# Even transforms of an FFT-and-FFN kernel: the middle chunk as two products of 64 rows, with a PSUM bank for each sum

## The chip, the cores and the metric

The kernel runs on one core of a Trainium2 chip. The metric is the device time of one execution in microseconds (us). TensorE (PE, with its weight loads as PEld) multiplies, VectorE (DVE), ScalarE (ACT) and GpSimd (POOL) do the elementwise work, SyncE (SP) issues most transfers.

## The reference

A two-dimensional FFT of a real array of 8 x 3072 x 256, of which the real part is kept, and a feed-forward layer on its 24,576 rows, all in 32-bit floats:

```python
def _attn_ref(x):
    X = np.fft.fft(x, axis=1)
    X = np.fft.fft(X, axis=2)
    return X.real.astype(np.float32)

def _moe_ref(x, w_in, w_out, alpha):
    h = x @ w_in                      # 256 -> 2048
    g = np.maximum(h, 0.0) + alpha * np.minimum(h, 0.0)
    return (g @ w_out).astype(np.float32)
```

## The kernel before, in words

The FFT along the features is folded into `w_in`, the one along the sequence is folded by symmetries and then done as products with tables of cosines and sines. Of each of the 8 batches come four blocks of 2 x 384 columns (386 in the first); each block goes through the feed-forward layer in 16 steps (`KF`), one for each 128 hidden features. So there are 64 steps to a batch, numbered r = 0 to 63, and s counts them through the whole program. The order of the work is written out by hand: a step emits `ffn1(s + 3)` (six products into two PSUM banks, lines 648 to 650, called q = 0 and q = 1 below), `ffn2(s)` (twelve products into the four accumulators `acc`, line 727) and `pair(s + 3)` with the elementwise work of the steps around it: DVE adds up `pf` (line 666) and `d` (line 673), ACT scales `d` back into the bank (line 677, tile `pq`), DVE makes `g` of both (line 631, in `split`), ACT rounds `g` to `hi` (line 633), POOL takes the rest `lo` (line 635). A bank of `ffn1` is free again when `split` has made its `g`.

Beside this, in each batch, the next batch's input is folded (`fold_piece`, r = 5 to 50) and transformed. The change is in the transforms of the even part, the *units* `see` (at r = 53), `cee` and then `ceo` (both at r = 57) and `seo` (r = 59); for batch 0 they stand in the prologue (`see`, `cee`) and at r = 10 and 11 (`ceo`, `seo`). A unit has three chunks of 128 rows of folded input, `fe[:, o]` to `fe[:, o + 2]`. The even sum needs the first chunk and half of the rows of the middle one, the odd sum the other half of the middle one and the last. Before, the middle chunk is multiplied twice with all 128 rows, with tables (`tab[:, 1]`, `tab[:, 2]`) whose other half is zero; so a unit has four products in 32-bit floats (`cee` a fifth, of the row `zres`), each of 192 or 193 columns, and both sums lie side by side in one bank (`ps`, line 510). Then `unit` calls `split` for the first bank of the step whose `g` is still open, ACT copies the odd sum to `os` (line 517), DVE makes `y` from the even sum plus and minus `os` (lines 525, 526), and ACT and POOL round `y` into `x` (lines 561, 562).

The four PSUM banks of the pool `pq` are shared by `ffn1` and the transforms. A new tile takes the bank whose release stands earliest in the program, and its first product waits for that release.

The 8-column case `m < P` of the same function (tile `f`) is the transform of one input column, done once for all batches.

Of the kernel before, what the change touches and what calls it, by code (L numbers as in the profile page):

```python
# [9 lines left out]
F32 = mybir.dt.float32  # L10
# [6 lines left out]
ACTF = mybir.ActivationFunctionType  # L17
ALU = mybir.AluOpType

NB, N, D, DFF = 8, 3072, 256, 2048  # L20
P = 128
# [92 lines left out]
def fft2_prelu_ffn(ctx: ExitStack, tc: tile.TileContext, t, out_a, out_b):  # L114
    nc = tc.nc
# [10 lines left out]
    pq = ctx.enter_context(tc.tile_pool(name="pq", bufs=4, space=PSUM))  # L126
    accp = ctx.enter_context(tc.tile_pool(name="accp", bufs=1, space=PSUM))
    ctx.enter_context(tc.manual_schedule())
    start = ctx.enter_context(ExitStack())
    st = start.enter_context(tc.tile_pool(name="st", bufs=1))  # L130

    V, S, G = nc.vector, nc.scalar, nc.gpsimd
# [10 lines left out]
    ee = tabs.tile([P, 9, 193], F32, name="ee")  # L143
# [63 lines left out]
    def other_bank():  # L207

        for s, i in list(st1):
            if i == 0 and s >= WHOLE:  # L210
                split(s, i)
        return pq.tile([P, 512], F32, tag="pq", name="ps")
# [145 lines left out]
    def fold_sums(i):  # L358

        b, c, h = PIECES[i]  # L360
        r = buf["x", i].rearrange("p (j i) s d -> p i s j d", i=2)
        ps = accp.tile([P, 512], F32, tag=f"acc{i % 4}", name="fold")
        for k in range(2):
            for n, (i_, s_) in enumerate(((0, 0), (0, 1), (1, 0), (1, 1))):
                nc.tensor.matmul(
                    out=ps[:, 256 * k:256 * k + 256], lhsT=ident[:, k * (i_ ^ s_)], rhs=r[:, i_, s_],
                    start=(n == 0), stop=(n == 3),
                )
        use("x", i)
        halves = ps.rearrange("p (k a j d) -> p k j a d", k=2, a=2, j=2)  # L370
        v = foldp.tile([P, 2, 2, 64], F32, tag="xeg", name="xeg")
        S.activation(out=v, in_=halves[:, :, 1], func=ACTF.Copy)
        return halves[:, :, 0], v
# [73 lines left out]
    TABS = dict(cee=ee[:, 0:4], see=ee[:, 5:9], ceo=eo[:, 0:4], seo=eo[:, 4:8])  # L447
# [44 lines left out]
    def dft(kind, half, fe, fo, zr, m, bank=None):  # L492

        ps = (bank or other_bank())[0:m]
        if kind in TABS:
            tab = TABS[kind]
            n = 193 if kind[1:] == "ee" else 192
            o = 0 if kind[1:] == "ee" else 3
            even = [(fe[:, o], tab[:, 0]), (fe[:, o + 1], tab[:, 1])]
            if kind == "cee":  # L500
                even.append((zr, ee[:, 4]))
            oddp = [(fe[:, o + 1], tab[:, 2]), (fe[:, o + 2], tab[:, 3])]
        else:
            n = 192
            sl = slice(half * 192, (half + 1) * 192)
            even = [(fo[:, q], odd[:, q, sl]) for q in range(3)]
            oddp = [(fo[:, 3 + q], odd[:, 3 + q, sl]) for q in range(3)]
        for o, terms in ((0, even), (n, oddp)):
            for i, (lhsT, rhs) in enumerate(terms):
                nc.tensor.matmul(  # L510
                    out=ps[:, o:o + n], lhsT=lhsT, rhs=rhs, start=(i == 0), stop=(i == len(terms) - 1),
                )
        return ps, n, m

    def odd_sums(ps, n, m):
        os = foldp.tile([P, 193], F32, tag="os", name="os", bufs=2)[0:m, 0:n]
        S.activation(out=os, in_=ps[:, n:2 * n], func=ACTF.Copy)
        return ps, os, n, m

    def butterfly(ps, n, m):  # L520
        return both_sums(*odd_sums(ps, n, m))

    def both_sums(ps, os, n, m, pool=foldp, tag="y"):
        y = pool.tile([P, WX], F32, tag=tag, name="y", bufs=1 if tag == "pf" else 2)[0:m, 0:2 * n]
        V.tensor_tensor(out=y[:, 0:n], in0=ps[:, 0:n], in1=os, op=ALU.add)
        V.tensor_tensor(out=y[:, n:2 * n], in0=ps[:, 0:n], in1=os, op=ALU.subtract)  # L526
        return y

    X = {}
# [8 lines left out]
    def unit_mm(b, kind, half, bank=None):  # L538
        s = 0 if kind[0] == "c" else 2
        fe, fo = (fold[b, "ce"], fold[b, "co"]) if s == 0 else (fold[b, "se"], fold[b, "so"])  # L540
        return dft(kind, half, fe, fo, zres, P, bank)
# [59 lines left out]
    def column_128_mm(kind, half):  # L601
        return dft(kind, half, f128, None, z128, NB)
# [190 lines left out]
    sums = {0: fold_sums(0)}  # L793
# [19 lines left out]
    fold_rest(4, *sums[4])  # L813
    weights_ih(0)
    x_sums = odd_sums(*column_128_mm("cee", 0))
    weights_mm(1)
    signs()
# [3 lines left out]
    fold_rest(5, *sums[5])  # L821
    weights_m(2, G)
    see_sums = odd_sums(*unit_mm(0, "see", 0))
    column_128_store("cee", 0, both_sums(*x_sums, pool=work, tag="pf"))
    load_xbc(0)
    weights_ih(1)
    weights_out(1)
    cee_sums = unit_mm(0, "cee", 0)
    y = both_sums(*see_sums)
    unit_store(0, "see", 0, G, y)  # L830
    cee_sums = odd_sums(*cee_sums)
    weights_c(1)
    y = both_sums(*cee_sums)
# [126 lines left out]
```

## Time and profile before

| | |
|---|---|
| median of 3 runs | 1796.56 us (1795.61 to 1797.21) |
| the profiled execution | 1797.46 us, its span 1795.7 us |
| PE busy | 99% of the span |
| DVE, POOL, ACT busy | 86%, 75%, 65% |
| share of the chain that ended last | PE 95% |
| mean granted TensorE clock | 0.997 of full speed |

Busy shares are of the whole span. The chain is followed back from the last instruction to what released each step. PE's records overlap, since products are pipelined: the distance from one start to the next is what a product costs in a row of them, not its own duration.

### The profile page before, as it was taken

What the parts mean: (1) busy time and instruction counts of PE and PEld (TensorE: products, weight loads), DVE (VectorE), ACT (ScalarE), POOL (GpSimd) and SP (SyncE); (2) the same over time, 40 slices, a digit from 0 to 9 for tenths busy, and PEclk for the clock granted to TensorE, in tenths of its full rate; (3) what the DMA queues carried; (4) which work ended last, traced back from release to release, by engine and by line L of the source; (5) the groups of instructions that cost most, each with busy time, mean ns of one, the idle gap of its engine ahead of it and who ended that gap; (6) DMA issues with size and microseconds to landing.
All of it is one profiled execution on the core that took longest, in us unless ns stands there. A gap on an engine that the chain in (4) does not pass through costs nothing.

```text
span 1795.7 us, 31584 instructions
## 1 busy us (share of the span) xinstructions
PE 1775.4 (99%) x9969; PEld 1740.1 (97%) x9969; DVE 1538.5 (86%) x3033; ACT 1169.5 (65%) x2426; POOL 1345.3 (75%) x1534
## 2 busy tenths in 40 slices
PE   8999999999999999999999999999999999999999
PEld 7789999999999999999999999999999999999998
DVE  6978987999879897798987989789997999878886
ACT  5865666666666667666676666666666666666665
POOL 2369977888678887788777887778877888676665
PEclk9999999999999999999999999999999999999999
DMA  6410110110101100010100111001110100000000
GB/s 242 144 35 26 58 64 19 39 42 17 46 23 35 42 35 29 23 46 30 62 19 6 47 46 47 19 6 58 35 46 19 39 20 4 23 23 23 23 19 19
DMA packets 28764, 71.76 MB, mean 40 GB/s; under 512 B 6546, under 2 KB 11700, under 8 KB 28468
## 3 DMA queue, kind: packets, MB, share of 16 engines
q1 hardware_dynamic: 28020, 69.31, 11.3%
q8 instruction: 78, 1.28, 0.3%
q14 instruction: 90, 0.74, 0.1%
q10 hardware_dynamic: 576, 0.43, 0.1%
HBM read 44.45 MB, written 25.26 MB: 39 GB/s over the span
## 4 chain that ended last, share of the span: by engine, by line
PE 95%; DVE 2%; POOL 1%; issue 0%; ACT 0%; DVEq 0%; POOLq 0%; ACTq 0%
PE acc L727 58%; PE pq L648 10%; PE pq L649 10%; PE pq L650 10%; PE ps L510 3%; PE ps L467 2%; PE acc L714 2%; PE ps L289 1%; DVE g L631 1%; DVE d L673 0%; POOL lo L635 0%; DVE xev L356 0%; ACT hi L633 0%; DVE pf L666 0%; POOL w L258 0%
## 5 line engine op out<-in xcount | busy, mean ns | idle before, releaser
L635 POOL TENSOR_TENSOR lo<-g,hi 128x384 fp32r<-128x384 f32 (+1 forms) x996 | 1020.6, 1040 | 325.4 <-ACT hi L633 300.5
L633 ACT ACTIVATE hi<-g 128x384 fp32r<-128x384 f32 (+1 forms) x996 | 523.9, 526 | 477.7 <-DVE g L631 447.6
L631 DVE SCALAR_TENSOR_TENSOR g<-d,sg,pq 128x384 f32<-128x384 f32 (+1 forms) x996 | 605.7, 608 | 23.0 <-POOL lo L635 23.0
L677 ACT ACTIVATE pq<-d,sga 128x384 f32<-128x384 f32 (+1 forms) x996 | 568.4, 572 | 31.4 <-DVE d L673 31.2
L673 DVE TENSOR_TENSOR d<-pf,pq 128x384 f32<-128x384 f32 (+1 forms) x1024 | 558.8, 548 | 5.8 <-PE pq L650 0.2
L727 PE MATMUL acc<-hi,woh 128*128 128x384 f32 (+1 forms) x1992 | 511.0, 337 | 0.0
L666 DVE SCALAR_TENSOR_TENSOR pf<-xbc,w,pq 128x384 f32<-128x384 f32 (+1 forms) x512 | 313.4, 612 | 148.9 <-PE pq L650 143.9
L727 PE MATMUL acc<-hi,wol 128*128 128x384 f32 (+1 forms) x1992 | 436.4, 338 | 0.0
L727 PE MATMUL acc<-lo,woh 128*128 128x384 f32 (+1 forms) x1992 | 435.6, 338 | 0.0
L648 PE MATMUL pq<-x,wih 128*128 128x384 f32 (+1 forms) x1024 | 355.2, 347 | 8.9 <-DVE g L631 6.8
L727 PEld LDWEIGHTS acc<-hi,woh 128*128 128x128 f32 x1992 | 361.9, 188 | 0.0
L727 PEld LDWEIGHTS acc<-hi,wol 128*128 128x128 f32 x1992 | 357.9, 189 | 0.4
L727 PEld LDWEIGHTS acc<-lo,woh 128*128 128x128 f32 x1992 | 355.8, 188 | 0.0
L649 PE MATMUL pq<-x,wih 128*128 128x384 f32 (+1 forms) x1024 | 346.6, 338 | 0.2 <-DVE x L562 0.2
L650 PE MATMUL pq<-x,wil 128*128 128x384 f32 (+1 forms) x1024 | 345.6, 337 | 0.0
L648 PEld LDWEIGHTS pq<-x,wih 128*128 128x128 f32 x1024 | 192.9, 188 | 21.7 <-DVE g L631 17.5
L649 PEld LDWEIGHTS pq<-x,wih 128*128 128x128 f32 x1024 | 192.9, 188 | 0.7 <-DVE x L562 0.4
L650 PEld LDWEIGHTS pq<-x,wil 128*128 128x128 f32 x1024 | 193.3, 189 | 0.0
L562 POOL TENSOR_TENSOR x<-y,x 128x384 fp32r<-128x384 f32 (+2 forms) x67 | 64.4, 973 | 33.4 <-ACT x L561 33.4
L356 POOL TENSOR_TENSOR raw<-raw 128x512 f32<-128x512 f32 (+2 forms) x84 | 69.9, 832 | 0.0
L258 POOL TENSOR_TENSOR w<-we,wm 128x512 int32<-128x512 int32 x16 | 20.4, 1277 | 47.4 <-DVE wm L249 27.8
L561 ACT ACTIVATE x<-y 128x384 fp32r<-128x384 f32 (+2 forms) x68 | 33.2, 506 | 31.1 <-DVE y L526 20.7
(148 smaller groups left out, 994.5 us busy)
## 6 DMA issues: line engine op xcount, KB each, us to landing
raw<-in_xh SPq DMA_DIRECT2D x48, 512.0 KB, 3.5
out<-o SPq DMA_DIRECT2D x48, 384.0 KB, 2.3
raw<-in_w SPq DMA_DIRECT2D x16, 512.0 KB, 3.7
out<-o SPq DMA_DIRECT2D x16, 386.0 KB, 2.5
xbc<-xcd SPq DMA_DIRECT2D x24, 192.0 KB, 3.3
xbc<-xcd SPq DMA_DIRECT2D x8, 193.0 KB
odd<-in_odd SPq DMA_DIRECT2D x1, 1152.0 KB, 6.7
table<-in_odd SPq DMA_DIRECT2D x6, 192.0 KB, 3.2
```

What stands on the lines that cost most here:

```text
L356: yield size, lambda o=o, i0=i0, i1=i1, op=op: e.tensor_tensor(out=o, in0=i0, in1=i1, op=op)
L562: lo_engine.tensor_tensor(out=lo, in0=v, in1=hi.bitcast(F32), op=ALU.subtract)
L631: V.scalar_tensor_tensor(out=g, in0=d, scalar=sg[:, f:f + 1], in1=ad, op0=ALU.mult, op1=ALU.max)
L633: S.activation(out=hi, in_=g, func=ACTF.Copy)
L635: G.tensor_tensor(out=lo, in0=g, in1=hi.bitcast(F32), op=ALU.subtract)
L648: nc.tensor.matmul(out=t_, lhsT=wih[:, f, q], rhs=xh, start=True, stop=False)
L649: nc.tensor.matmul(out=t_, lhsT=wih[:, f, q], rhs=xl, start=False, stop=False)
L650: nc.tensor.matmul(out=t_, lhsT=wil[:, f, q], rhs=xh, start=False, stop=True)
L666: V.scalar_tensor_tensor(out=pf, in0=xbc[g], scalar=w128[:, f:f + 1], in1=ps[0], op0=ALU.mult, op1=ALU.add,)
L673: V.tensor_tensor(out=d, in0=pf, in1=ps[1], op=ALU.add if i else ALU.subtract)
L677: S.activation(out=ad, in_=d, func=ACTF.Copy, scale=sga[:, f:f + 1])
L727: nc.tensor.matmul(out=acc[o, i], lhsT=wt[:, f, o * P:(o + 1) * P], rhs=hl[i][part], start=(f == 0 and n[o] == 0), stop=(f == KF - 1 and n ...
```

## The change

For full units the middle chunk is multiplied once, as two products of 64 rows: rows 0 to 63 with `tab[0:64, 1]` into the even sum, rows 64 to 127 with `tab[64:128, 2]` into the odd sum. The two sums lie in a bank each, so that a unit now takes two tiles of the pool `pq`, and the first and last chunks are multiplied ahead of the middle one. The odd transforms of batch 0 and the 8-column case stay as they were (`side_by_side`).

```diff
-        for o, terms in ((0, even), (n, oddp)):
+        two = ps[:, 0:n], pq.tile([P, 512], F32, tag="pq", name="ps")[:, 0:n]
+        first, second = [(fe[:, o], tab[:, 0])] + res, [(fe[:, o + 2], tab[:, 3])]
+        for out, terms in zip(two, (first, second)):
             for i, (lhsT, rhs) in enumerate(terms):
-                nc.tensor.matmul(
-                    out=ps[:, o:o + n], lhsT=lhsT, rhs=rhs, start=(i == 0), stop=(i == len(terms) - 1),
-                )
-        return ps, n, m
+                nc.tensor.matmul(out=out, lhsT=lhsT, rhs=rhs, start=(i == 0), stop=False)
+        for i, out in enumerate(two):
+            sl = slice(64 * i, 64 * i + 64)
+            nc.tensor.matmul(out=out, lhsT=fe[sl, o + 1], rhs=tab[sl, 1 + i], start=False, stop=True)
+        return two, n, m
...
     def odd_sums(ps, n, m):
         os = foldp.tile([P, 193], F32, tag="os", name="os", bufs=2)[0:m, 0:n]
-        S.activation(out=os, in_=ps[:, n:2 * n], func=ACTF.Copy)
+        S.activation(out=os, in_=ps[1], func=ACTF.Copy)
         return ps, os, n, m
...
-        V.tensor_tensor(out=y[:, 0:n], in0=ps[:, 0:n], in1=os, op=ALU.add)
-        V.tensor_tensor(out=y[:, n:2 * n], in0=ps[:, 0:n], in1=os, op=ALU.subtract)
+        V.tensor_tensor(out=y[:, 0:n], in0=ps[0], in1=os, op=ALU.add)
+        V.tensor_tensor(out=y[:, n:2 * n], in0=ps[0], in1=os, op=ALU.subtract)
```

The orders of instructions on DVE, ACT, POOL and SP stay as they were. On PE the number of products stays too, but their waits move. At `see` of batch 1 (r = 53 of batch 0) PE had, before (a row is a line, an operation, out<-in, its size, and the engines whose semaphores it waits for):

```order
L727 MATMUL acc<-lo,woh 128x384 x2
L510 MATMUL ps<-ee,fse 128x193 [waits DVE_49]
L510 MATMUL ps<-ee,fse 128x193 x3
L648 MATMUL pq<-x_1415,wih 128x384 [waits DVE_49]
L649 MATMUL pq<-x_1415,wih 128x384
L650 MATMUL pq<-x_1415,wil 128x384
L648 MATMUL pq<-x_1415,wih 128x384 [waits DVE_49]
```

And at the same place it has now (line 514 is a chunk of 128 rows, line 517 a half of 64 rows, lines 660 to 662 are what 648 to 650 were, 739 what 727 was):

```order
L739 MATMUL acc<-lo,woh 128x384 x2
L514 MATMUL ps<-ee,fse 128x193 [waits DVE_49] x2
L517 MATMUL ps<-ee,fse 128x193 x2
L660 MATMUL pq<-x_1419,wih 128x384 [waits DVE_49]
L661 MATMUL pq<-x_1419,wih 128x384
L662 MATMUL pq<-x_1419,wil 128x384
L660 MATMUL pq<-x_1419,wih 128x384 [waits Activation_49]
```

The unit has taken the two banks that the next `ffn1` had. Its q = 0 now goes into the bank freed by the `split` that `unit` itself emits (before, q = 1 did), and q = 1 into the bank of the unit's odd sum, which ACT frees with the copy `os`. At `cee` and `ceo` of the same batch PE had, before:

```order
L510 MATMUL ps<-ee,fce 128x193 [waits DVE_49]
L510 MATMUL ps<-ee,fce 128x193
L510 MATMUL ps<-ee,zres 128x193 [waits DMAHW1_49]
L510 MATMUL ps<-ee,fce 128x193 x2
L510 MATMUL ps<-eo,fce 128x192 [waits DVE_49]
L510 MATMUL ps<-eo,fce 128x192 x3
L648 MATMUL pq<-x_1415,wih 128x384 [waits DVE_49]
```

And now:

```order
L514 MATMUL ps<-ee,fce 128x193 [waits DVE_49]
L514 MATMUL ps<-ee,zres 128x193 [waits DMAHW1_49]
L514 MATMUL ps<-ee,fce 128x193 [waits DVE_49]
L517 MATMUL ps<-ee,fce 128x193 x2
L514 MATMUL ps<-eo,fce 128x192 [waits DVE_49]
L514 MATMUL ps<-eo,fce 128x192 [waits Activation_49]
L517 MATMUL ps<-eo,fce 128x192 x2
L660 MATMUL pq<-x_1419,wih 128x384 [waits DVE_49]
L661 MATMUL pq<-x_1419,wih 128x384
L662 MATMUL pq<-x_1419,wil 128x384
L660 MATMUL pq<-x_1419,wih 128x384 [waits Activation_49]
```

The second product of `ceo` now goes into the bank of the odd sum of `cee` and waits for its copy on ACT; the q = 0 behind it waits for the `y` of `cee` on DVE, and the q = 1 for the copy of the odd sum of `ceo`.

## Rows read from the trace of the kernel before

**Rows 1.** The page: busy time of the engines, and the chain that ended last, by engine.

```profile
PE 1775.4 (99%) x9969; PEld 1740.1 (97%) x9969; DVE 1538.5 (86%) x3033; ACT 1169.5 (65%) x2426; POOL 1345.3 (75%) x1534
...
PE 95%; DVE 2%; POOL 1%; issue 0%; ACT 0%; DVEq 0%; POOLq 0%; ACTq 0%
```

**Rows 2.** The chain that ended last in order of time, around the units of the last batch: start us, us, engine, tile, line.

```profile
1549.03 1.31 PE ps L510 x8
...
1562.96 2.94 PE ps L510 x18
```

**Rows 3.** The records of line 510 for one table and input: count, duration in ns (min/median/max), first and last start in us.

```profile
L510 PE MATMUL ps<-ee,fse x64: 324/326/431, 27.8 to 1550.0; 128*128 128x193 f32 x64
```

**Rows 4.** The timeline around `see` of the last batch: start us, us, engine, line, operation, out<-in, count, and in brackets the idle time before it.

```profile
1548.43 0.61 DVE L631 SCALAR_TENSOR_TENSOR g<-d,sg,pq 128x384 f32<-128x384 f32 x1
...
1548.87 1.47 PE L510 MATMUL ps<-ee,fse 128*128 128x193 f32 x8
...
1549.79 0.61 DVE L631 SCALAR_TENSOR_TENSOR g<-d,sg,pq 128x384 f32<-128x384 f32 x1 [0.29 <-POOL lo L635]
...
1550.04 0.48 PE L648 MATMUL pq<-x,wih 128*128 128x384 f32 x1
...
1550.36 0.34 PE L649 MATMUL pq<-x,wih 128*128 128x384 f32 x1
...
1550.50 0.53 ACT L633 ACTIVATE hi<-g 128x384 fp32r<-128x384 f32 x1 [0.37 <-DVE g L631]
...
1550.71 0.34 PE L648 MATMUL pq<-x,wih 128*128 128x384 f32 x1
...
1550.93 0.31 ACT L517 ACTIVATE os<-ps 128x193 f32<-128x193 f32 x1
...
1551.27 0.36 DVE L525 TENSOR_TENSOR y<-ps,os 128x193 f32<-128x193 f32 x1 [0.87 <-ACT os L517]
```

**Rows 5.** The timeline around `cee` and `ceo` of the last batch, the same columns.

```profile
1562.80 0.82 PE L510 MATMUL ps<-ee,fce 128*128 128x193 f32 x4
...
1563.27 0.61 DVE L631 SCALAR_TENSOR_TENSOR g<-d,sg,pq 128x384 f32<-128x384 f32 x1 [0.29 <-POOL lo L635]
...
1563.78 0.82 PE L510 MATMUL ps<-ee,fce 128*128 128x193 f32 x4
...
1564.43 1.46 PE L510 MATMUL ps<-eo,fce 128*128 128x192 f32 x8
...
1564.63 0.33 ACT L517 ACTIVATE os<-ps 128x193 f32<-128x193 f32 x1
...
1565.28 0.35 DVE L526 TENSOR_TENSOR y<-ps,os 128x193 f32<-128x193 f32 x1
...
1565.66 0.53 ACT L561 ACTIVATE x<-y 128x386 fp32r<-128x386 f32 x1 [0.69 <-DVE y L526]
...
1566.09 0.31 ACT L517 ACTIVATE os<-ps 128x192 f32<-128x192 f32 x1
...
1566.26 0.34 PE L648 MATMUL pq<-x,wih 128*128 128x384 f32 x1
```

**Rows 6.** The timeline around `seo` of the last batch, the same columns.

```profile
1572.04 1.46 PE L510 MATMUL ps<-eo,fse 128*128 128x192 f32 x8
...
1572.49 0.61 DVE L631 SCALAR_TENSOR_TENSOR g<-d,sg,pq 128x384 f32<-128x384 f32 x1 [0.29 <-POOL lo L635]
...
1573.20 0.52 ACT L633 ACTIVATE hi<-g 128x384 fp32r<-128x384 f32 x1 [0.37 <-DVE g L631]
...
1573.63 0.31 ACT L517 ACTIVATE os<-ps 128x192 f32<-128x192 f32 x1
...
1573.86 0.34 PE L648 MATMUL pq<-x,wih 128*128 128x384 f32 x1
```

**Rows 7.** The timeline behind `see` of batch 1, where PE does wait for a `g`: the `g`, the weight load that waits for it, and the product after the next.

```profile
256.42 0.61 DVE L631 SCALAR_TENSOR_TENSOR g<-d,sg,pq 128x384 f32<-128x384 f32 x1 [0.28 <-POOL lo L635]
...
257.09 0.19 PEld L648 LDWEIGHTS pq<-x,wih 128*128 128x128 f32 x1 [0.53 <-DVE g L631]
...
257.37 0.34 PE L649 MATMUL pq<-x,wih 128*128 128x384 f32 x1
```

**Rows 8.** The timelines of PE and PEld around the 8-column products (`eo,f`), which use a part of the array's columns: the last of them, and the products of 128 columns behind them.

```profile
94.96 1.47 PE L510 MATMUL ps<-eo,f 128*8 128x192 f32 x8
...
96.36 0.19 PEld L648 LDWEIGHTS pq<-x,wih 128*128 128x128 f32 x1 [0.33 <-issue]
...
96.64 0.34 PE L649 MATMUL pq<-x,wih 128*128 128x386 f32 x1
```

**Rows 9.** The timelines of PE and ACT in the prologue, at `see` and `cee` of batch 0.

```profile
29.63 0.59 PE L510 MATMUL ps<-ee,fse 128*128 128x193 f32 x2 [0.64 <-DVE fse L394]
...
30.27 0.33 ACT L517 ACTIVATE os<-ps 128x193 f32<-128x193 f32 x1 [2.59 <-PE ps L510]
...
31.96 0.33 ACT L517 ACTIVATE os<-ps 128x193 f32<-128x193 f32 x1
32.19 0.68 ACT L238 ACTIVATE wt<-raw 128x512 bf16<-128x512 bf16 x1
```

**Rows 10.** Who waited for whom, over the whole span: us in total, times, the longest.

```profile
DVE pf L666 <- PE pq L650: 143.9, 291, 1.3
...
PEld pq L648 <- DVE g L631: 17.5, 34, 2.8
```

More of the change, by code (lines that the diff above doesn't have):

```diff
@@ L494, in dft @@
         ps = (bank or other_bank())[0:m]
[L495 to L503, printed above, removed]
+        if kind not in TABS:
             n = 192
@@ L507, in dft, with side_by_side @@
             oddp = [(fo[:, 3 + q], odd[:, 3 + q, sl]) for q in range(3)]
-        for o, terms in ((0, even), (n, oddp)):
-            for i, (lhsT, rhs) in enumerate(terms):
-                nc.tensor.matmul(
-                    out=ps[:, o:o + n], lhsT=lhsT, rhs=rhs, start=(i == 0), stop=(i == len(terms) - 1),
-                )
-        return ps, n, m
+            return side_by_side(ps, n, even, oddp)
+        tab = TABS[kind]
+        n = 193 if kind[1:] == "ee" else 192
+        o = 0 if kind[1:] == "ee" else 3
+        res = [(zr, ee[:, 4])] if kind == "cee" else []
+        if m < P:
+            even = [(fe[:, o], tab[:, 0]), (fe[:, o + 1], tab[:, 1])] + res
+            oddp = [(fe[:, o + 1], tab[:, 2]), (fe[:, o + 2], tab[:, 3])]
+            return side_by_side(ps, n, even, oddp)
+        two = ps[:, 0:n], pq.tile([P, 512], F32, tag="pq", name="ps")[:, 0:n]
+        first, second = [(fe[:, o], tab[:, 0])] + res, [(fe[:, o + 2], tab[:, 3])]
+        for out, terms in zip(two, (first, second)):
+            for i, (lhsT, rhs) in enumerate(terms):
+                nc.tensor.matmul(out=out, lhsT=lhsT, rhs=rhs, start=(i == 0), stop=False)
[3 more added lines that the diff above has]
+        return two, n, m
+    def side_by_side(ps, n, *sums):
+        two = ps[:, 0:n], ps[:, n:2 * n]
+        for out, terms in zip(two, sums):
+            for i, (lhsT, rhs) in enumerate(terms):
+                nc.tensor.matmul(out=out, lhsT=lhsT, rhs=rhs, start=(i == 0), stop=(i == len(terms) - 1))
+        return two, n, ps.shape[0]
     def odd_sums(ps, n, m):
         os = foldp.tile([P, 193], F32, tag="os", name="os", bufs=2)[0:m, 0:n]
-        S.activation(out=os, in_=ps[:, n:2 * n], func=ACTF.Copy)
+        S.activation(out=os, in_=ps[1], func=ACTF.Copy)
         return ps, os, n, m
```

## The prediction

> **What bounds the kernel now.** I read the page first: PE is busy for 99% of the span and makes up 95% of the chain that ended last [rows 1]. Then the chain in order of time around the units: it runs through PE without a gap, a unit with 1.31 us of its own, the pair `cee` and `ceo` with 2.94 us [rows 2]. So what a unit takes from PE, or what PE waits at it, is time of the kernel, unless PE would have waited soon after anyway. Then the timelines of the three places of a batch, to see which releases lie close to PE.
>
> **Terms of the working.** The 64 records of one table and input are two for each of 8 batches x 4 products: a product in 32-bit floats is two passes, each with weights of its own [rows 3]. Eight passes of `see` take 1.47 us, the last one 0.326, so they follow each other after (1.47 - 0.326) / 7 = 0.163 us [rows 3, 4]; the products of `ffn1` after 0.175 us (0.35 for two) [rows 4]. Times below are from a place's first pass. Where PE must wait for another engine, the next product starts 0.16 us behind the end of what it waits for: the `g` ended at 256.42 + 0.61 = 257.03, the load started at 257.09, and the product at 257.37 - 0.175 = 257.19 [rows 7].
>
> **Part 1: four passes less of zeros.** Two products of 128 rows (four passes) become two of 64 rows (four passes again). If the two halves run side by side, the second half's first pass lies beside the first half's second one, and the four passes take three distances: 0.163 us less for a unit. If not, nothing is gained. No row of before has products of 64 rows; the bounds are 0 and 0.163 us, and I take 0.163, since the halves lie in different rows and have banks of their own. The Trainium skill, "TensorE: Matmul & The Clock Gate", Part 3 on packing small matmuls, has products in different row strips run at the same time, with starts some 4 ns apart but in program order; by it the gain is the 0.163, without it the rival *one after another* below.
>
> **Part 2: the array set to halves and back.** The nearest rows are the 8-column products, which use a part of the columns. Their last pass starts at 94.96 + 1.47 - 0.326 = 96.10 and leaves room for the next at 96.27. The next weight load starts only at 96.36, with nothing to wait for ("issue"), and its product at 96.64 - 0.175 = 96.46 [rows 8]. So 0.19 us are lost on the way back: about 0.1 until the load starts, 0.1 for the load that is no longer ahead. I take 0.2 us for each change of setting, two in a unit, and 0 as the other bound (rows may be different from columns). The Trainium skill, "TensorEngine Tiling (Array Packing)", Key Properties, says that changing the tiling mode, as against the tile, drains the engine. By that rule both changes cost and the sum is the one below; if none costs, the sum is that of *free settings*. Rows 8 agree with it for columns; no row here shows it for rows.
>
> **Part 3: the waits for banks.** The unit takes two banks, so the next `ffn1` gets for q = 0 the bank of the `g` that `unit` itself asks for, and for q = 1 the unit's odd bank, freed by the copy `os`. ACT's order is unchanged: `os` still stands behind the `hi` of that `g`.
>
> *See.* Before, q = 1 starts at 1550.71 - 1548.87 = 1.84. Now q = 0 waits for the `g` that ends at 1.53 and starts at 1.69; q = 1 waits for `os`, which ends at 2.37 (it is behind `hi`, not behind PE: PE is done earlier), and starts at 2.53 [rows 4]. That is **+0.69 us**, whatever parts 1 and 2 give: with them PE would be ready for q = 0 at 4 x 0.163 + 0.2 + 3 x 0.163 + 0.2 = 1.54. Behind q = 1 stand only PE's own instructions; DVE needs them at about the same time, since its `y` starts at 2.40 and keeps it busy.
>
> *Seo.* q = 0 at 1.54, q = 1 three products later at 2.07. The copy still starts behind `hi`, at 1.59, ends at 1.90 and would allow 2.06. Before: 1.82 [rows 6]. **+0.25 us.**
>
> *Cee and ceo.* Six full passes to 0.98, setting 1.18, halves to 1.67. The last pass of `cee` starts at 1.51 and ends at 1.83; `os` follows 0.03 us later (1564.60 to 1564.63 in the rows) and ends at 2.19. `ceo`: setting 1.87, first product to 2.20, the second must wait for that `os` until 2.35 and ends at 2.68; setting 2.88, halves to 3.37, setting, q = 0 at 3.57, q = 1 at 4.10. The `y` of `cee` ends at 2.83 and the second `os` at 3.88, both in time. Before, q = 1 starts at 3.46 [rows 5]. **+0.64 us.**
>
> **Sum.** Seven batches x (0.69 + 0.25 + 0.64) = 11.1 us. Batch 0: `ceo` has no wait that binds, 0.2 + 0.2 - 0.16 = 0.24; `seo` between this and the 0.69 of a copy that is waited for, 0.4. Prologue: behind the late DVE rows two passes start at 29.73, so the last half starts at 29.73 + 0.33 + 0.2 + 0.33 = 30.59, and `os` at 30.94 instead of 30.27; the one of `cee` by the same steps at 32.82 instead of 31.96, and ACT's preparation of weights stands behind it [rows 9]: 0.9 if all of it arrives, which I take, 0 if the loads of weights hide it. Together 11.1 + 0.24 + 0.4 + 0.9 = 12.6 us. On the profiled execution that is 1797.46 + 12.6 = 1810.1; the median of the runs is 0.9 lower, so **1809.2 us**, 0.7% slower. `os` and `y` cost what they did, reading the same columns.
>
> **The rivals.** Runs of one kernel differ by some 0.1%, so I call 0.2% (3.6 us) about what can be told from no change.
>
> *One after another* (settings cost, halves don't overlap): `see` stays 0.69, `seo` 0.41, `cee` and `ceo` 0.97; 2.07 x 7 = 14.5, with batch 0 and the prologue (0.4 + 0.5 + 1.2) 16.6: 1813.2. Speaks for it that all passes of one kind follow each other one by one in rows 4; against it, the separate banks.
>
> *Free settings, halves overlap*: `see` 0.69, `seo` 0.24, both held by `os`. `cee` ends at 1.47, its `os` at 1.99, `ceo` goes on at 2.15 and ends at 2.96; its own `os`, behind ACT's `x` [rows 5], ends at about 3.47, q = 1 at 3.63: +0.17. 1.10 x 7 = 7.7 and 0.4 for batch 0 and the prologue: 8.1, 1804.7. Against it stand rows 8.
>
> *Free settings, one after another*: 0.69 + 0.24 + 0.51 = 1.44, x 7 = 10.1, and 0.8: 10.9, 1807.5. The change would then not do what it says, and only the banks' waits were left.
>
> *A setting costs a whole record more* (some 0.4 us each): 0.2 more at each of the six in `seo`, `cee` and `ceo` of a batch, 1.2 x 7 = 8.4 and 1 at the start on top of 12.6: 22 us, 1818.6.
>
> *Given back*: PE's weight loads wait 17.5 us in 34 places for a `g`; a PE that is later would wait less there, and nothing measurable is left: 1796.6. Against it: DVE waits 143.9 us for PE's `ffn1` [rows 10], so it follows PE more than it leads, and behind the units the chain is PE alone [rows 2].
>
> *Faster*: the overlap pays and the copies are in time. The place is q = 1 behind `see`: it decides whether `os` ends before 1.68 instead of at 2.37. Then only the passes count, 32 x 0.163 = 5.2 us less: 1791.3. Against it, ACT's order behind `hi` [rows 4].
>
> **How the numbers follow.** The forecast 0.42; one after another 0.17; free and overlapping 0.17; free and one after another 0.10; dearer settings 0.05; given back 0.05; faster 0.04. The first four hold 0.86 and lie between 1804.7 and 1813.2; with a little for the steps of the prologue the range is 1803 to 1815. All cases but the last two are slower by more than 0.2%: slower 0.91, same 0.05, faster 0.04.
>
> **What would show it.** In the profile after: the chain of waits has PE's `ffn1` line waiting for ACT `os` 14 to 22 times, each at or behind a unit, some 0.3 us at `see`. At `see` q = 0 starts near 1.7 and q = 1 near 2.5 us behind the first pass; at `ceo` the second product starts about 0.15 us late. The records of the halves tell part 1 (starts of the second half's first and the first half's second pass together, or 0.163 apart), and the start of the first weight load of the halves and of the next `ffn1` tells part 2 (0.1 us behind the room that the last pass leaves, or one pass ahead as elsewhere). I am wrong if those loads stay ahead, if PE's waits behind later units shrink by what was lost at the unit, or if `os` starts earlier because `hi` does.

## The result, and the profile after

The changed kernel takes 1807.38 us (median of 4 runs, 1806.23 to 1811.69) against 1796.88 for the kernel before on the same chip: 1.0066 times as long, 95% interval 1.0054 to 1.0079. The profiled execution takes 1807.74 us, its span is 1806.0 us; both are 10.3 us more than in the profile before.

The page of the changed kernel, busy time and the chain by engine, answers to [rows 1]:

```profile
PE 1782.8 (99%) x9969; PEld 1726.7 (96%) x9969; DVE 1538.5 (85%) x3033; ACT 1171.2 (65%) x2426; POOL 1345.1 (74%) x1534
...
PE 90%; DVE 3%; ACT 2%; POOL 2%; issue 1%; DVEq 0%; POOLq 0%; ACTq 0%
```

PE is as busy by share, but it has lost 5 points of the chain to the other engines: they are now waited for on the way to the end. Who waited for whom (us in total, times, the longest), in answer to [rows 10]:

```profile
DVE pf L678 <- PE pq L662: 154.5, 298, 1.3
...
PEld pq L660 <- DVE g L643: 23.0, 49, 2.7
...
PEld ps L517 <- issue: 7.2, 32, 0.2
...
PEld pq L660 <- ACT os L529: 4.1, 14, 0.4
PEld ps L514 <- issue: 3.5, 9, 1.7
...
PEld ps L514 <- ACT os L529: 1.4, 7, 0.2
```

The `g` is waited for 15 times more than before. The copy `os` is waited for 14 times by `ffn1` (line 660) and 7 times by a whole chunk of a unit (line 514); before, PE never waited for it. The first weight load of the halves (line 517) sits idle 32 times, once in each unit, 0.22 us each, for nothing the profile shows. A whole chunk behind the halves (line 514) has the same idle load; the longest of its waits, 1.7 us, lies in the prologue, where the rows of `fse` come late. And DVE waits 10.6 us more for PE's `ffn1`: PE's lateness goes on to DVE.

The timeline around `see` of the last batch, changed kernel, in answer to [rows 4] (start us, us, engine, line, operation, in brackets the idle time before):

```profile
1557.94 0.82 PE L514 MATMUL ps<-ee,fse 128*128 128x193 f32 x4
...
1558.69 0.30 PEld L517 LDWEIGHTS ps<-ee,fse 64*128 64x128 f32 x4 [0.23 <-issue]
1558.69 0.60 PE L517 MATMUL ps<-ee,fse 64*128 64x193 f32 x4
1558.86 0.61 DVE L643 SCALAR_TENSOR_TENSOR g<-d,sg,pq 128x384 f32<-128x384 f32 x1 [0.28 <-POOL lo L647]
1559.53 0.19 PEld L660 LDWEIGHTS pq<-x,wih 128*128 128x128 f32 x1 [0.54 <-DVE g L643]
...
1559.57 0.53 ACT L645 ACTIVATE hi<-g 128x384 fp32r<-128x384 f32 x1 [0.36 <-DVE g L643]
...
1560.00 0.32 ACT L529 ACTIVATE os<-ps 128x193 f32<-128x193 f32 x1
...
1560.37 0.19 PEld L660 LDWEIGHTS pq<-x,wih 128*128 128x128 f32 x1 [0.36 <-ACT os L529]
...
1560.65 0.34 PE L661 MATMUL pq<-x,wih 128*128 128x384 f32 x1
```

Of the four half passes, the two that have started by 1558.72 us:

```profile
1558.69 0.43 PE L517 MATMUL ps<-ee,fse 64*128 64x193 f32 x2
```

Together they take 0.43 us, the longest that one of them takes alone (428 ns): two passes start together, then the other two.

The load of q = 0 starts 0.06 us behind the end of the `g`, the load of q = 1 0.05 us behind the end of `os`, which stood behind `hi` on ACT. A product whose load is not ahead is recorded from the start of that load; its own place in the row is 0.175 us ahead of the next one. So q = 1 stands at 1560.65 - 0.175 - 1557.94 = 2.53 us behind the unit's first pass. Before it was 1.84: +0.69.

`cee` and `ceo` of the last batch, in answer to [rows 5]:

```profile
1572.55 0.49 PE L514 MATMUL ps<-ee,fce 128*128 128x193 f32 x2
...
1573.62 0.30 PEld L517 LDWEIGHTS ps<-ee,fce 64*128 64x128 f32 x4 [0.23 <-issue]
...
1574.14 0.30 PEld L514 LDWEIGHTS ps<-eo,fce 128*128 128x128 f32 x2 [0.23 <-issue]
...
1574.26 0.33 ACT L529 ACTIVATE os<-ps 128x193 f32<-128x193 f32 x1
...
1574.65 0.30 PEld L514 LDWEIGHTS ps<-eo,fce 128*128 128x128 f32 x2 [0.20 <-ACT os L529]
...
1575.17 0.30 PEld L517 LDWEIGHTS ps<-eo,fce 64*128 64x128 f32 x4 [0.23 <-issue]
...
1576.32 0.34 PE L660 MATMUL pq<-x,wih 128*128 128x384 f32 x1
```

The second product of `ceo` waits for the copy of `cee`, as the order said it would, and q = 1 stands 1576.32 - 1572.55 = 3.77 us behind the first pass; before 1566.26 - 1562.80 = 3.46: +0.31.

`seo` of the last batch, in answer to [rows 6]:

```profile
1582.11 0.81 PE L514 MATMUL ps<-eo,fse 128*128 128x192 f32 x4
...
1582.85 0.30 PEld L517 LDWEIGHTS ps<-eo,fse 64*128 64x128 f32 x4 [0.23 <-issue]
...
1583.69 0.31 ACT L529 ACTIVATE os<-ps 128x192 f32<-128x192 f32 x1
...
1584.34 0.34 PE L661 MATMUL pq<-x,wih 128*128 128x384 f32 x1
```

q = 1 stands at 1584.34 - 0.175 - 1582.11 = 2.06, before 1.82: +0.24. The chain in order of time (start us, us, line, passes), in answer to [rows 2], shows what the array itself takes:

```profile
1572.71 0.98 PE ps L514 x6
1573.69 0.53 PE ps L517 x4
1574.22 1.02 PE ps L514 x4
1575.24 0.53 PE ps L517 x4
...
1582.27 0.65 PE ps L514 x4
1582.92 0.53 PE ps L517 x4
```

Six whole passes take 0.98 and four 0.65 (0.163 each, as before); four half passes with the change of setting ahead of them take 0.53. The 1.02 of the whole chunks of `ceo` are 0.65, a change of setting and the wait for the copy of `cee`.

The lateness adds up over the program. The first pass of a unit, changed kernel against before, from one execution of each:

| unit | start before, us | later by, us |
|---|---|---|
| `see`, batch 0 | 27.84 | 0.04 |
| `ceo`, batch 0 | 100.11 | 0.55 |
| `seo`, batch 0 | 105.05 | 0.62 |
| `see`, batch 1 | 254.89 | 0.79 |
| `cee`, batch 1 | 269.35 | 1.55 |
| `seo`, batch 1 | 278.59 | 1.88 |
| `see`, batch 7 | 1548.87 | 9.07 |
| `cee`, batch 7 | 1562.80 | 9.75 |
| `seo`, batch 7 | 1572.04 | 10.07 |
| end of the span | 1795.7 | 10.3 |

A single step of this table is only as good as one execution. The kernel with one pair of units (below) has the code of the kernel before up to r = 57 of batch 0; still its stretch from `seo` of batch 0 to `see` of batch 1 is 0.8 us longer than before.

### The profile page after: what moved, and what is told of

Read it like the earlier page. It is cut to its first block, busy times and chain, and to the rows that moved or that the text cites. A ratio compares the mean times of both kernels' runs of the same rounds, so it can differ in the third digit from the quotient of the medians.

```text
span 1806.0 us, 31548 instructions
## 1 busy us (share of the span) xinstructions
PE 1782.8 (99%) x9969; PEld 1726.7 (96%) x9969; DVE 1538.5 (85%) x3033; ACT 1171.2 (65%) x2426; POOL 1345.1 (74%) x1534
## 4 chain that ended last, share of the span: by engine, by line
PE 90%; DVE 3%; ACT 2%; POOL 2%; issue 1%; DVEq 0%; POOLq 0%; ACTq 0%
PE acc L739 55%; PE pq L660 10%; PE pq L661 9%; PE pq L662 9%; PE ps L467 2%; PE acc L726 2%; POOL lo L647 1%; PE ps L514 1%; DVE g L643 1%; PE ps L517 1%; ACT hi L645 1%; PE ps L289 1%; DVE d L685 0%; ACT pq L689 0%; PE ps L524 0%
## 5 line engine op out<-in xcount | busy, mean ns | idle before, releaser
L660 PE MATMUL pq<-x,wih 128*128 128x384 f32 (+1 forms) x1024 | 356.5, 348 | 10.6 <-DVE g L643 8.3
```

The source lines that it names most:

```text
L660: nc.tensor.matmul(out=t_, lhsT=wih[:, f, q], rhs=xh, start=True, stop=False)
```

## The experiments

**The banks alone.** The changed kernel, but the middle chunk multiplied twice with all rows, so that only the second bank is left of the change:

```diff
-        first, second = [(fe[:, o], tab[:, 0])] + res, [(fe[:, o + 2], tab[:, 3])]
-        for out, terms in zip(two, (first, second)):
+        even = [(fe[:, o], tab[:, 0]), (fe[:, o + 1], tab[:, 1])] + res
+        oddp = [(fe[:, o + 1], tab[:, 2]), (fe[:, o + 2], tab[:, 3])]
+        for out, terms in zip(two, (even, oddp)):
...
-        for i, out in enumerate(two):
-            sl = slice(64 * i, 64 * i + 64)
-            nc.tensor.matmul(out=out, lhsT=fe[sl, o + 1], rhs=tab[sl, 1 + i], start=False, stop=True)
```

> The banks alone: the four (five) products of a unit with all 128 rows, as before, but even and odd sums in a bank each. If the waits for the banks make the loss (theory): behind see the q = 1 of ffn1 starts at 2.53 us from the unit's first pass instead of 1.84 (+0.69), behind seo +0.25, behind cee and ceo about +0.3; seven batches x 1.24 = 8.7 us and 0.1 to 0.5 in batch 0, nothing in the prologue: 1805.3 to 1806.5 against 1796.6. If the loss comes from setting the array to halves and back (rival), this kernel is level with before (within 1 us).

Measured: 1806.75 us, before 1797.32 on that chip (this one serves the next three runs too): ratio 1.0057 (1.0043 to 1.0071), 9.4 us more. PE's waits in this kernel, where 658 is the first line of `ffn1`, 515 that of the units and 527 the copy:

```profile
PEld pq L658 <- DVE g L641: 19.6, 38, 2.9
PEld pq L658 <- ACT os L527: 6.8, 21, 0.4
...
PEld ps L515 <- ACT os L527: 0.7, 1, 0.7
```

`os` is waited for 21 times, three in each of seven batches: behind `see`, behind `ceo` and behind `seo`. In the timelines of the last batch q = 1 stands at 2.55, 3.77 and 2.06 us, within 0.02 of the changed kernel. So the second bank is enough for most of the loss by itself; in the changed kernel the halves with their settings lie under the waits at `see` and `seo`. At `cee` and `ceo` the same 3.77 is a coincidence: here it comes from the wait of q = 1 for the second copy, there from four changes of setting less the overlap (0.15 us) and the wait of `ceo`'s second product for the first copy (0.17). In the prologue, where I expected nothing, this kernel loses 0.6 us between `see` and `cee`, whose first product waits for the copy of `see` (line 515). The intervals of the two kernels overlap, so the 1 us between them is not a finding.

**One half, one bank.** The kernel before, in which the middle product of the even sum takes 64 rows alone (its table's other half is zero); everything stays in one bank and in its order:

```diff
-            even = [(fe[:, o], tab[:, 0]), (fe[:, o + 1], tab[:, 1])]
+            rows = slice(0, 64) if m == P else slice(0, P)
+            even = [(fe[:, o], tab[:, 0]), (fe[rows, o + 1], tab[rows, 1])]
```

> The array's setting alone: one bank a unit as before; only the even sum's middle product has 64 rows, the odd sum's middle product keeps 128 rows, so there are two changes of setting in a unit, no two halves side by side, and no new wait. If each change costs 0.2 us as read from the changed kernel's records (theory), a unit is 0.40 us longer: 28 units x 0.4 = 11.2 us and up to 1.6 in the prologue and batch 0's four units: 1807.8 to 1809.4. If the waits for banks make all of the loss and the setting is free (rival), it is level with before.

Measured: 1808.24 us, ratio 1.0064 (1.0049 to 1.0080), 10.9 more. `seo` of the last batch, of which [rows 6] shows the 1.46 us of before:

```profile
1582.44 1.85 PE L511 MATMUL ps<-eo,fse 128*128 128x192 f32 x8
...
1582.86 0.29 PEld L511 LDWEIGHTS ps<-eo,fse 64*128 64x128 f32 x2 [0.23 <-issue]
...
1583.37 0.62 PEld L511 LDWEIGHTS ps<-eo,fse 128*128 128x128 f32 x4 [0.23 <-issue]
```

The same eight passes take 0.39 us longer, and the load sits idle for 0.23 us twice: into the half, and out of it. Between `seo` of batch 1 and of batch 7 this kernel loses 9.1 us, 0.38 for each of the 24 units. A change of setting by rows therefore costs 0.195 us, as the way back from 8 columns in [rows 8] (0.19); the rivals with free settings are out. Alone the settings lose as much as the whole change does: the two losses, 9.4 and 10.9, do not add up in the changed kernel, because there the overlap pays most of the settings back and, at `see` and `seo`, what is left lies under the waits. By the Trainium skill, "TensorEngine Tiling (Array Packing)", Key Properties, a change of the tiling mode drains the engine; the 0.23 us of idle load at both changes are in keeping with it, though no row shows the array empty.

**The second half in the same rows.** The changed kernel with both half products in rows 0 to 63; it leaves out rows 64 to 127 of the middle chunk:

```diff
-            nc.tensor.matmul(out=out, lhsT=fe[sl, o + 1], rhs=tab[sl, 1 + i], start=False, stop=True)
+            nc.tensor.matmul(out=out, lhsT=fe[0:64, o + 1], rhs=tab[0:64, 1 + i], start=False, stop=True)
```

> The changed kernel with one edit: the second half product reads rows 0 to 63 too, as the first does, so both lie in the same rows of the array (its odd sums leave out rows 64 to 127 of the middle chunk and take rows 0 to 63 with the tables' zeros in their place). Theory: the halves run side by side because they lie in different rows; here they run one after another, four half passes take four distances instead of two, 0.327 us more in each unit: see stays as it is (held by os), seo has its q = 1 at 2.23 us instead of 2.06 (+0.17), cee and ceo +0.65 together, so 7 x 0.82 = 5.7 us, with batch 0 and the prologue some 6.5 over the changed kernel: about 1814. Rival (the two banks alone let them run beside each other): no change to the changed kernel, 1807.

Measured: 1811.41 us, before 1796.12 on that chip (which also serves the two runs on the copy's order and the whole pairs): ratio 1.0087 (1.0073 to 1.0100), 15.3 more. `seo` of the last batch, the loads and products of the halves:

```profile
1585.61 0.62 PEld L517 LDWEIGHTS ps<-eo,fse 64*128 64x128 f32 x4 [0.23 <-issue]
1585.61 0.91 PE L517 MATMUL ps<-eo,fse 64*128 64x192 f32 x4
```

And the same four passes in the chain:

```profile
1585.68 0.84 PE ps L517 x4
```

Four loads now take 0.62 us instead of 0.30, the four passes 0.91 instead of 0.59, and 0.84 of the chain instead of 0.53: some 0.32 us more, two distances. So the overlap comes from the different rows, not from the banks. `see` keeps its 2.42 us to the record of q = 1 (held by `os`), `cee` and `ceo` take 1579.08 - 1574.66 = 4.42 to q = 1, 0.65 more than in the changed kernel, as expected, and `seo` 0.16 more. Between `seo` of batch 1 and of batch 7 this kernel loses 1.98 us to a batch against the kernel before, the changed kernel 1.37; the difference of 0.61 is less than the 0.82 that I expected, and the time accordingly (4 to 5 us over the changed kernel instead of 6.5; the intervals of the two overlap, so it is the rows above that carry the reading). Of the 1.3 us that are missing over these six batches some 0.56 lie in one stretch, from `seo` of batch 4 to `see` of batch 5, which is no larger than what single executions differ by elsewhere; the rest I did not follow.

**The copy ahead of `hi`.** The changed kernel, with `os` ahead of the rounding of `g` on ACT:

```diff
-        sums = unit_mm(b, kind, half, pq.tile([P, 512], F32, tag="pq", name="ps"))
+        sums = odd_sums(*unit_mm(b, kind, half, pq.tile([P, 512], F32, tag="pq", name="ps")))
...
-        unit_store(b, kind, half, lo_engine, butterfly(*sums))
+        unit_store(b, kind, half, lo_engine, both_sums(*sums))
```

> The changed kernel with one edit: the unit's copy os is emitted ahead of the split's rounding hi on ACT. Theory (the waits for os make most of the loss): at see os ends 0.7 us earlier, q = 1 starts at about 2.2 us behind the first pass instead of 2.53 (+0.38 over before instead of +0.69), at seo at 1.90 instead of 2.06 (+0.08 instead of +0.24), cee and ceo keep their +0.33. 7 x 0.79 = 5.5, and 0.8 for batch 0 and the prologue: 6.3 us over the kernel before, about 1803, some 4 us under the changed kernel. Rival (the loss is the array's, or hi is late in its place): no change to the changed kernel, 1807.

Measured: 1801.71 us, ratio 1.0034 (1.0022 to 1.0046), 5.6 more than before; nearly half of the loss is gone by the order of two instructions. `see` of the last batch:

```profile
1552.88 0.84 PE L514 MATMUL ps<-ee,fse 128*128 128x193 f32 x4
...
1553.82 0.61 DVE L643 SCALAR_TENSOR_TENSOR g<-d,sg,pq 128x384 f32<-128x384 f32 x1 [0.28 <-POOL lo L647]
1554.29 0.33 ACT L529 ACTIVATE os<-ps 128x193 f32<-128x193 f32 x1
1554.48 0.19 PEld L660 LDWEIGHTS pq<-x,wih 128*128 128x128 f32 x1 [0.53 <-DVE g L643]
...
1554.52 0.52 ACT L645 ACTIVATE hi<-g 128x384 fp32r<-128x384 f32 x1
...
1555.12 0.33 PE L660 MATMUL pq<-x,wih 128*128 128x384 f32 x1
```

The copy ends ahead of need, and q = 1 stands at 2.24 instead of 2.53 (+0.40 over before), in `seo` at 1.90 (+0.08), in `cee` and `ceo` at 3.79 (+0.33): 0.38, 0.08 and 0.33 were expected. What is left at `see` is the wait of q = 0 for the `g`, at which its load starts 0.05 us behind. So q = 0 still has the bank of that `g`, though the copy that frees the odd bank now stands ahead of it in the program. The rule that a new tile takes the bank whose release stands earliest does not hold here as I told it; what decides instead no run shows.

**Two units, one excursion.** If a change of setting costs 0.2 us and a pair of halves saves 0.327, one unit cannot win and two that share the two changes can. Both even sums go into one bank and both odd sums into another, with whole chunks of the first unit, halves of the first, halves of the second, whole chunks of the second; the open `g` are all asked for ahead of the pair, so no `ffn1` waits for a copy. First `cee` and `ceo` alone, then `see` and `seo` too (both at r = 53):

```diff
+        whole_rows(True)
+        for k, (kind, o, n, sl) in enumerate(sums):
+            for i, bank in enumerate((one, two)):
+                r = slice(64 * i, 64 * i + 64)
+                nc.tensor.matmul(
+                    out=bank[:, sl], lhsT=fe[r, o + 1], rhs=TABS[kind][r, 1 + i], start=(k == 1), stop=(k == 0),
+                )
+        whole_rows(False)
+        for s, i in list(st1):
+            split(s, i)
...
+                if r == 53:
+                    unit_pair(b + 1, ("see", "seo"), G)
+                if r == 57:
+                    unit_pair(b + 1, ("cee", "ceo"), G)
```

> cee and ceo of batches 1 to 7 together: both even sums in one bank, both odd sums in the other, the four halves in one stretch between the first unit's whole products and the second's, and both open g made at once, so that ffn1 behind it waits for neither copy. Ten whole passes (1.63), two changes (0.4), four distances of halves side by side (0.65): 2.69 us against 2.94 of before, 0.25 less, x 7 = 1.8 us less: 1794.9. If the halves save only one distance a unit (what the prediction took), 3.0 us: 0.5 us slower in all. If the copies or the earlier g hold up PE (rival): 2 us or more slower than before.

> The same for see and seo too, both at r = 53. Eight whole passes (1.31), two changes (0.4), four distances (0.65) are 2.36 us against 2 x 1.31 = 2.62: 0.26 less, with the pair of cee and ceo 0.51 less a batch, x 7 = 3.6 us less: 1793.0. At r = 53 DVE is later than at r = 57, its second g ends about 2.5 us behind the first pass, still ahead of q = 1 at 2.89. If that g or the two copies come too late (rival), the gain of this pair is gone, and the kernel is level with the one that pairs cee and ceo alone, or slower.

Measured: one pair 1795.30 us, ratio 0.9989 (0.9980 to 0.9998); both pairs 1794.10 us, ratio 0.9983 (0.9974 to 0.9992), 3.2 us under the kernel before. The chain of the kernel with both pairs, at `see` and `seo` of the last batch:

```profile
1546.30 0.67 PE ps L553 x4
1546.97 0.85 PE ps L562 x8
1547.82 0.85 PE ps L553 x4
```

Eight half passes take 0.85 with the change ahead of them (four distances and 0.2), the whole chunks behind them 0.85 with the change back: 2.37 us where the kernel before has 2 x 1.31 [rows 2], 0.25 less. Twice 0.25 in seven batches are 3.5, against the 3.2 measured.

**The same pairs without halves.** The control, with the middle chunks multiplied twice by all rows:

```diff
+        for kind, o, n, sl in sums:
+            tab = TABS[kind]
+            even = [(fe[:, o], tab[:, 0]), (fe[:, o + 1], tab[:, 1])]
...
+            oddp = [(fe[:, o + 1], tab[:, 2]), (fe[:, o + 2], tab[:, 3])]
```

> The control of e4_pairs: its pairs, its banks and its early g, but the middle chunks multiplied twice with all 128 rows, as before the change; no halves, no setting of the array. Theory: the gain of e4_pairs comes from the passes that lie beside each other in the halves, so here the pairs cost what they cost before (see with seo 2.62 us, cee with ceo 2.94), no copy is waited for, and the time is level with the kernel before: 1797, within 1 us of it. Rival: the gain comes from the new order (both open g ahead of the pair, see moved next to seo) and not from the halves: about 3 us under the kernel before, 1794.

Measured: 1796.03 us, ratio 0.9998 (0.9990 to 1.0007): level with the kernel before. The interval just touches that of both pairs with halves (0.9974 to 0.9992), so the chain has to carry the reading, at `see` with `seo` and at `cee` with `ceo` of the last batch:

```profile
1547.98 2.61 PE ps L554 x16
...
1563.18 2.94 PE ps L554 x18
```

These are the 2 x 1.31 and the 2.94 of the kernel before [rows 2]; with halves the first of them took 2.37. The gain of the pairs is that of the halves, not of the new order.

## Why the prediction was right

The sign came out, and the cause and the size in the main: 12.6 us forecast, 10.3 to 10.5 measured, inside the range. The time alone proves little: three of the rivals lie in the range too, and 1807.4 is nearer to the 1807.5 of *free settings, one after another* than to the forecast's 1809.2. What tells them apart are the rows and the runs above. By the steps:

- **Part 3, the banks**, was right where it stood alone. `see`: forecast +0.69, measured +0.69, with `os` behind `hi` and q = 1 at 2.53. `seo`: forecast +0.25, measured +0.24, and here the number was luck: I had PE ready for q = 1 only at 2.07, beside a copy that allows 2.06; with the larger overlap PE would be ready at 1.90, where q = 1 stands in the run with the copy ahead, and it is the copy alone that holds it at 2.06. `ffn1` waits for `os` 14 times, where 14 to 22 were announced. The kernel with the banks alone loses 9.4 us; the one with the copy ahead of `hi` gets back 0.29 us at each `see` and 0.16 at each `seo`.
- **Part 2, the settings**: 0.2 us each was right, 0.195 in the kernel with one half. That this held for rows as for columns was a choice between two ends, and nothing in the trace of before could show it. The dearer settings (0.4 us each) fall with it.
- **Part 1, the halves**, is the step that was mis-sized. I let the second half's first pass lie beside the first half's second one, and so saved one distance, 0.163 us. In the trace the four passes take two distances: the chain's 0.53 less 0.2 for the setting is 0.33, and the four loads start within 0.30 - 0.18 = 0.12 us of each other. Eight halves in a row (0.85) take 0.32 more than four (0.53), which gives the two distances without taking the setting for known. Neither of the two signs that I had named came: two passes start together and then two more, and since passes in the same rows follow each other (the run with both halves in rows 0 to 63), each pair is one pass of either half. The gain is 0.327 a unit. With it a unit costs 0.4 - 0.327 = 0.07 us more on the array, not 0.24.
- **`cee` and `ceo`** inherit this twice: 0.64 - 2 x 0.163 = 0.31, the measured value. The wait of `ceo`'s second product was there, with a copy that ended 0.15 us earlier than I had it.
- **The start**: I had 0.9 us for the prologue, 0.24 and 0.4 for `ceo` and `seo` of batch 0. The table shows 0.51, 0.07 and 0.17. The 0.07 of `ceo` is its 0.24 less the overlap; the 0.17 holds the whole way to batch 1, on which single executions of the same code differ by more, and says nothing. The prologue's delay of ACT was smaller than the 0.9 that I took, and all of it arrives at the first `ffn1`, which waits for ACT's `x`. Its weight load before:

```profile
34.63 0.19 PEld L648 LDWEIGHTS pq<-x,wih 128*128 128x128 f32 x1 [2.06 <-ACT x L561]
```

The copy of `cee` (before: 31.96, [rows 9]) and that load in the changed kernel:

```profile
32.66 0.33 ACT L529 ACTIVATE os<-ps 128x193 f32<-128x193 f32 x1 [0.21 <-PE ps L517]
...
35.32 0.19 PEld L660 LDWEIGHTS pq<-x,wih 128*128 128x128 f32 x1 [1.88 <-ACT x L573]
```

Less the 0.04 by which `see` started later, the copy is 0.66 late and the load 0.65, where my sum had 0.86 for the copy; 0.51 is left at `ceo`.

Put together: 0.79 us up to batch 1 instead of 1.54, and 10.3 - 0.79 = 9.5 us in seven batches instead of 11.1. The measured terms give 7 x (0.69 + 0.24 + 0.31) = 8.7 of these 9.5. Of the remaining 0.8 some 0.55 lies in two stretches between units of one batch and the next (278 to 471 us and 1141 to 1333 us). That is within what single executions differ by: the kernel with one pair, whose code is that of the kernel before there, gains 0.7 us in the second of them. So the 0.8 is neither explained nor told from noise.

Of the rivals, *one after another* is the kernel with both halves in the same rows: 15.3 us, where its sum was 16.6. Both *free settings* fell with the 0.39 us of the kernel with one half. *Given back* fell with the growth in the table: nearly all of a unit's loss is still there at the next one, and PE's waits for a `g`, which should have shrunk, grew from 17.5 to 23.0 us. *Faster* needed the copy in time; even then the changed kernel would not win, as the run with the copy ahead of `hi` shows: q = 0 still waits for the `g`, and the settings take more than the overlap gives.

## What to carry to other kernels

Before splitting a product into halves of the array, count the changes of setting beside the passes saved: here an excursion to halves and back costs 0.4 us and a pair of halves in different rows saves 0.33, so one unit loses 0.07 by it and two that share an excursion win 0.25. Both figures are for 192 or 193 columns; other widths were not run. A tile taken from a pool that others use costs what its release waits for: look up which engine frees the bank that the next user gets, and what stands ahead of that release in that engine's order. Where a copy frees a bank that is waited for and a rounding does not, the copy goes first: here that was worth some 5 us.

## What was not expected of the hardware

Two products of 64 rows in 32-bit floats run pass beside pass: the four weight loads take 0.30 us from the first start to the last end, where four in the same rows take 0.62, and the four products have 0.33 us of the chain instead of 0.65. The Trainium skill, "TensorE: Matmul & The Clock Gate", Part 3, says that products in different row strips run at once and start in program order a few ns apart; the trace agrees with the first, also for products that are two passes each. In which order the passes of the two halves were issued the records don't say, so whether the compiler or the engine interleaves them stays open.

The other finding is that the change by rows costs 0.2 us in either direction (in the kernel with both pairs 0.85 instead of 0.65 for the four whole passes behind the halves), as much as the way back from an 8-column tile in [rows 8]. No row of before could tell this.
